# Gated linear attention with a spatially gated MLP: more kinds of work for ScalarE and GpSimd, and a new order of the whole program

## The chip, the cores and the metric

The kernel runs on one core of one Trainium2 chip. The metric is the device time of one execution in microseconds (us). The profile's names are used for the engines: PE is TensorE's matrix array, DVE is VectorE, ACT is ScalarE, POOL is GpSimd, SP is SyncE, which here only issues transfers (DMAs).

## The reference, cut to what matters

Batch 4, 8 heads, 768 steps, head size 40. The recurrent attention (below) feeds an MLP of 320 -> 1024 -> 320 columns with a mixing matrix over the 768 steps. All is float32.

```python
for t in range(S):
    m_new = np.maximum(f_gate[:, :, t] + m, i_gate[:, :, t])
    f_stab, i_stab = np.exp(f_gate[:, :, t] + m - m_new), np.exp(i_gate[:, :, t] - m_new)
    C = f_stab * C + i_stab * einsum('bhd,bhe->bhde', vt, kt)
    n = f_stab * n + i_stab * kt
    denom = np.maximum(np.abs(n . qt), 1.0)
    y[:, :, t] = sigmoid(o_gate[:, :, t]) * (C qt) / denom
h = np.maximum(x @ w_in, 0.0);  u, v = h[..., :512], h[..., 512:]
v_n = (v - mean(v)) / np.sqrt(var(v) + 1e-06)
v_s = einsum('ts,bsd->btd', w_spatial, v_n) + b_spatial
out = (u * v_s) @ w_out
```

## The kernel before, in words

The recurrence is computed in blocks of 128 steps for all 8 heads: 6 blocks a batch row, 24 blocks, numbered n = 0 to 23. Jobs are named by a short word and the number of the block:

- `s` (scores k.q, line 539), `ex` and `ebm` (the exponents of the decay as small matmuls, 542 and 551), on PE; `W` and `Eb` take their exponentials on ACT (554, 553).
- `ks` (two DVE products of `s` and `W`, 64 rows each) and `q` (two products of queries and `Eb`, on DVE or POOL) build the left operand of the output matmul. `kt` multiplies the keys by the last column of `W` (line 582); `dc` (PE, 578 and 580) makes from them what the block adds to the state; `c1`, `d1`, `d2`, `c2` carry the state on.
- `pv` (PE, 606 and 607) gives numerator and denominator. `da` takes twice the absolute denominator, `den` clamps it and takes the reciprocal (616, 617), `xm` multiplies `th` (the tanh form of the output gate) plus one by it (634), `xg` multiplies the numerator in, `xd` copies 64 columns, `px` (PE, 653) transposes, `xh` and `xl` store the result as a high and a low part, which together keep float32 in PE's fp32r format.
- In the MLP `V` (PE, 691) makes v, and `re`, `sq`, `va`, `po`, `nb`, `vn`, `vh`, `vl` normalise and split it; `pu` (733) and `u` make u; `pb` (743 to 745) is the mixing; `g`, `gu`, `gh`, `gl` gate and split; `c` (766 to 768) is the last matmul, `oc` and `out` copy and store. Names here carry batch row, half or block, and quarter: `V00`, `pu001`.

The weights must be split into high and low parts too. The input matrix comes in five pieces (`wi01`, `wi2`, `wi11`, `wi10`, `wi00`) whose words were viewed as 64-bit pairs, so the kernel first puts floats together: `_t` shifts one word right by 29 (line 427), `_x` rescales the other on ACT (429), `_b` merges both (431), `_h` rounds to the high part, `_l` takes the difference. The output matrix (`wo0` to `wo3`) goes the same way, the mixing matrix (`ws`) needs only `_h` and `_l`.

The gates are prepared on 32 partitions in three pieces of time, z = 0, 1, 2 (128, 256 and 384 steps): scan `m`, additions `fa`, `fs`, `is`, `as`, scan `g`, splits `gh`, `gl`, `ah`, `al`, nearly all on DVE. For block 0 four tiny transfers `dg0` to `dg3` and one `da` (same word as the denominator's job, without a number) carry them to the operands of `ex0`.

The order is written out by hand: the table ORDER lists every job, and each engine carries out its jobs in that order, one after the other. A suffix (`:V`, `:A`, `:P`) puts a job on DVE, ACT or POOL; without one the first engine in the job's list of alternatives takes it (a list like `dict(POOL=0.78, DVE=0.49)`, whose numbers are planned costs that the run does not use). Transfers go through the queues of SP and ACT in the same order, and a queue waits at the head for what its next transfer needs. Buffers come from pools (for instance 8 PSUM banks, 3 for q and k) and are handed out along the same table.

```python
job(f"kt{n}", dict(POOL=0.78, DVE=0.49), self.tt(...))
job(f"den{n}", dict(DVE=0.4), den1, w=[den], due=D0 + 6)
job(f"xm{n}", dict(POOL=1.85, DVE=0.485), gate, ...)
```

Of the kernel before, what the change touches and what calls it, by code (L numbers as in the profile page):

```python
# [9 lines left out]
F32 = mybir.dt.float32  # L10
# [3 lines left out]
AF = mybir.ActivationFunctionType  # L14
# [26 lines left out]
    ident=([128, 128], F32), warm=([128, 1], F32), half_neg=([128, 1], F32),  # L41
# [8 lines left out]
half_neg ident rhz1:V f1:A i0:S ey0:V f0:A rhz2:V i1 mk1 f2:A m0 wi01_ld cg0 mk0 i2 rst0 fa0 rst1 fs0 wi2_ld:A is0 g0 qk0:A m1 ca0 s0 gh0 dg1:A gl0 as0 wi01_t rhz0 dg0  # L50
rh0_1 ah0 rh0_0 fa1 dg2:A al0 wi2_x da dg3:A m2 fs1 wg0 wi2_t is2 is1 ex0 wi2_b wi11_ld:A g1 fa2 wi02_h as1 cg1 ah1 fs2 al1 gh1 qk1 W0 wi01_x wa1 cz0:V gl1 wg1 ks0_1
ks0_0 rh1_1:A ebm0 Eb0 kt0 dc0 ra01:A qk2 g2 wi01_b gm1 c1_0:A qz rh1_0 s1 as2 q0_1:V pv0 wi11_x gh2 gm2:A wi11_t ebm1 wi02_l wi10_ld d2_0 ex1 gl2 wi11_b ah2 th0 wg2 da0
den0 al2 wi11_h Eb1 W1 wa2 rh2_0 kt1 s2 dc1 wi10_x xm0:V wi11_l c2_0 ks1_0 rh2_1 gm3 qk3 wi00_ld d1_1:P xg0 ra02 xd0 ks1_1 ex2 c1_1 wi10_t q1_1:V q1_0 wi12_h eg01 ebm2
px0 wi10_b Eb2 th1 wi12_l xh0 xl0 wi10_h pv1 rh3_1:A da1 eg00 ebm3 gm4 eg11 W2 d2_1 qk4:A Eb3 wi10_l den1 kt2 xm1:V V00 ks2_1 xg1 rh3_0 ex3 c2_1 ks2_0 wi00_t wi00_x xd1
d1_2 q3_0:V wi00_b q2_1:V q2_0 rh4_0 px1 ebm4 xh1 rh4_1 W3 ex4 W4 wi01_h kt3 re00 dc2 c1_2 s3 d2_2:P pv2 xl1 dc3 s4 wi01_l:P da2 Eb4 gm6 gm5 th2 ks3_0 V01 ks3_1 c2_2 d1_3
qk5 ey1 den2 c1_3 ws00_ld:A ebm5 xm2:V we0 ex5 ks4_1 ca1 d2_3:P wa0 xg2 kt4 c2_3 q3_1:V ra10 xd2 rh5_1 ks4_0 q4_0:V d1_4:P wi00_h px2 eg20 gm7:A eg10 W5 q4_1:V dc4 s5 pv3
c1_4 xh2 pv4 sq00 th4 th3 xl2 ks5_1 we1 d2_4:P V02 ks5_0 wi00_l:P va00:V qk6:A re01 da3:V wo0_ld:A Eb5 rh5_0 pu001 ws00_h ex6 den3 xm3:V re02 c2_4 q5_0:V da4 ra11 th5
den4 eg21 po00 sq01 W6 rh6_0 pu002 pu000 xm4:V rh6_1:A u001 kt5:V q5_1:V eb7_1 xg4 xd4:V px4 dc5 va01:V qk7 xg3 nb00 d1_5 xd3:P vn00 s6 vh00:V xh4 c1_5 xl4 vl00 wo0_x
eb6_0 u000 sq02 pv5 ks6_1 da5:V ra22:A px3 po01 den5 va02:V ws00_l:P nb01:V V04 xh3 ex7 xl3 xm5:V po02 vn01 ks6_0 ws02_ld eb6_1 ws01_ld re04 xg5 W7 nb02:V u002 cz6 q6_1
xd5:V eb7_0:A V03 px5 vn02 sq04 kt6:V dc6 s7 c1_6:A va04 po04 xh5 nb04 ws01_h vh02 vn04 gm9 wo3_ld pv6 ws02_h:V gm8 xl5 vh01:V ks7_1 da6 re03 ks7_0 V05 vl01 vh04:V vl04  # L60
ws02_l:P ws01_l:P wo1_ld rh7_0 vl02 sq03 re05 va03 po03 pb0030 th6 pu003 sq05 va05 po05 nb05 pb0031 wo1_t we2 pb0032 ra12 d2_6:P u003 nb03:V wo1_x vn03 rh8_0 q7_1:V
# [145 lines left out]
class Kernel:  # L207
# [294 lines left out]
    def attention(self, n):  # L502
# [334 lines left out]
```

## Time and profile before

| | us |
|---|---|
| three runs, median (lowest to highest) | 348.05 (347.5 to 350.71) |
| the profiled execution, its own time | 346.94 |
| its span, first to last instruction | 345.2 |
| PE busy in the span | 326.2 |
| DVE / ACT / POOL busy | 257.6 / 130.7 / 108.7 |

A matmul's end is modelled, so a busy PE is not PE at its peak; the distance from one start to the next says at which rate it works. Idle time is put down to what released the waiting instruction.

### The profile page before, as it was taken

What the parts mean: (1) busy time and instruction counts of PE and PEld (TensorE: products, weight loads), DVE (VectorE), ACT (ScalarE), POOL (GpSimd) and SP (SyncE); (2) the same over time, 40 slices, a digit from 0 to 9 for tenths busy, and PEclk for the clock granted to TensorE, in tenths of its full rate; (3) what the DMA queues carried; (4) which work ended last, traced back from release to release, by engine and by line L of the source; (5) the groups of instructions that cost most, each with busy time, mean ns of one, the idle gap of its engine ahead of it and who ended that gap; (6) DMA issues with size and microseconds to landing.
All of it is one profiled execution on the core that took longest, in us unless ns stands there. A gap on an engine that the chain in (4) does not pass through costs nothing.

```text
span 345.2 us, 9069 instructions
## 1 busy us (share of the span) xinstructions
PE 326.2 (95%) x3654; PEld 303.7 (88%) x3654; DVE 257.6 (75%) x545; ACT 130.7 (38%) x312; POOL 108.7 (32%) x154
## 2 busy tenths in 40 slices
PE   0499999999899999999999999999999999999995
PEld 0387788899899989999999989999999999999995
DVE  5999998789997979865569657696946785536471
ACT  1455576961541166550221146640112227402011
POOL 6123553746643013434051005440233612100000
PEclk9999999999999999999999999999999999999999
DMA  6879658878373493250703674242061000100012
GB/s 194 229 213 264 175 161 226 213 160 225 120 226 99 130 230 91 62 150 0 211 26 96 177 184 113 68 124 78 10 160 38 0 3 21 58 0 2 0 40 76
DMA packets 17866, 40.12 MB, mean 116 GB/s; under 512 B 4212, under 2 KB 7860, under 8 KB 17824
## 3 DMA queue, kind: packets, MB, share of 16 engines
q1 hardware_dynamic: 12048, 26.49, 28.1%
q10 hardware_dynamic: 5616, 12.94, 13.8%
q8 instruction: 29, 0.48, 0.6%
q0 software_dynamic: 160, 0.11, 0.2%
q14 instruction: 13, 0.11, 0.1%
HBM read 35.09 MB, written 4.42 MB: 114 GB/s over the span
## 4 chain that ended last, share of the span: by engine, by line
PE 71%; DVE 4%; issue 1%; ACT 1%
PE pu L733 11%; PE pm L691 10%; PE pb L743 9%; PE pb L745 8%; PE pb L744 8%; PE pc L766 4%; PE pc L768 4%; PE pc L767 4%; PE pv L606 4%; PE s L539 3%; PE dc L578 2%; PE px L653 2%; DVE pb L255 1%; DVE KS L255 1%; PE pv L607 1%
## 5 line engine op out<-in xcount | busy, mean ns | idle before, releaser
L743 PE MATMUL pb<-wsH,v 128*128 128x384 f32 x192 | 65.6, 342 | 0.2 <-DVE KS L255 0.2
L745 PE MATMUL pb<-wsH,v 128*128 128x384 f32 x192 | 64.7, 337 | 0.0
L744 PE MATMUL pb<-wsL,v 128*128 128x384 f32 x192 | 64.6, 337 | 0.0
L539 PE MATMUL s<-QK 40*64 40x64 f32 x768 | 29.6, 232 | 10.2 <-DMA QK<-in_qk 10.2
L743 PEld LDWEIGHTS pb<-wsH,v 128*128 128x128 f32 x192 | 36.1, 188 | 0.9 <-issue 0.5
L744 PEld LDWEIGHTS pb<-wsL,v 128*128 128x128 f32 x192 | 36.1, 188 | 0.5
L255 DVE TENSOR_TENSOR KS<-s,W 64x512 f32<-64x512 f32 x48 | 33.0, 688 | 4.6 <-PE s L539 2.3
L745 PEld LDWEIGHTS pb<-wsH,v 128*128 128x128 f32 x192 | 36.0, 188 | 0.0
L539 PEld LDWEIGHTS s<-QK 40*64 40x64 f32 x768 | 26.4, 145 | 10.6 <-DMA QK<-in_qk 10.2
L255 DVE TENSOR_TENSOR pb<-pb,bsp 128x384 f32<-128x384 f32 x32 | 17.7, 562 | 22.3 <-PE pb L745 22.2
L733 PE MATMUL pu<-xH,wiH 128*128 128x384 f32 x96 | 32.9, 342 | 0.6 <-ACT W L554 0.6
L733 PE MATMUL pu<-xL,wiH 128*128 128x384 f32 x96 | 32.3, 336 | 0.0
L259 ACT CAST gt<-pb 128x384 fp32r<-128x384 f32 x21 | 10.0, 481 | 57.2 <-DVE pb L255 49.4
L766 PE MATMUL pc<-woH,gt 128*128 128x320 f32 x96 | 30.5, 318 | 0.0
L255 POOL TENSOR_TENSOR KS<-QK,Eb 64x512 f32<-64x512 f32 (+1 forms) x21 | 27.7, 1318 | 8.1 <-PE pc L768 6.2
L691 PE MATMUL pm<-wiH,xH 128*128 128x512 f32 x72 | 29.9, 416 | 0.0
L767 PE MATMUL pc<-woL,gt 128*128 128x320 f32 x96 | 29.7, 309 | 0.0
L768 PE MATMUL pc<-woH,gt 128*128 128x320 f32 x96 | 29.6, 309 | 0.0
L691 PE MATMUL pm<-wiH,xL 128*128 128x512 f32 x72 | 29.0, 403 | 0.0
L607 PE MATMUL pv<-RH,KS 128*64 128x41 f32 x384 | 27.4, 237 | 1.2 <-DVE RH L255 0.7
L606 PE MATMUL pv<-RH,KS 104*64 104x41 f32 x384 | 27.8, 238 | 0.4 <-DVE gt L255 0.4
L606 PEld LDWEIGHTS pv<-RH,KS 104*64 104x64 f32 x384 | 25.4, 145 | 2.8 <-issue 1.2
(124 smaller groups left out, 761.5 us busy)
## 6 DMA issues: line engine op xcount, KB each, us to landing
RH<-in_vk SPq DMA_DIRECT2D x35, 256.0 KB
QK<-in_qk SPq DMA_DIRECT2D x15, 448.0 KB
QK<-in_qk ACTq DMA_DIRECT2D x9, 448.0 KB
RH<-in_vk ACTq DMA_DIRECT2D x13, 256.0 KB
out<-o SPq DMA_DIRECT2D x14, 160.0 KB
wsr<-in_w_sp SPq DMA_DIRECT2D x5, 384.0 KB
out<-o ACTq DMA_DIRECT2D x10, 160.0 KB
wir<-in_w_in SPq DMA_DIRECT2D x3, 512.0 KB
```

The lines of the kernel that those rows point to most:

```text
L255: return lambda e: e.tensor_tensor(out=out(), in0=in0(), in1=in1(), op=op)
L539: self.nc.tensor.matmul(o[64 - p0:128 - p0, h], q[p0:p0 + D, 0, h], q[p0:p0 + D, 1, h], start=True, stop=True)
L606: self.nc.tensor.matmul(o[0:64, h], ks[0:ke, 0, h], v0[0:ke, h], start=True, stop=True)
L607: self.nc.tensor.matmul(o[64:128, h], ks[:, 1, h], v1[:, h], start=True, stop=True)
L691: self.nc.tensor.matmul(pmt(), l, r, start=i == 0, stop=i == len(terms) - 1)
L733: self.nc.tensor.matmul(put(), w, x, start=i == 0, stop=i == len(terms) - 1)
L743: self.nc.tensor.matmul(pbt(), vH[:, cd], wh[:, s], start=s == 0, stop=False)
L744: self.nc.tensor.matmul(pbt(), vH[:, cd], wl[:, s], start=False, stop=False)
L745: self.nc.tensor.matmul(pbt(), vL[:, cd], wh[:, s], start=False, stop=s == NB - 1)
L766: self.nc.tensor.matmul(pct(), gH[:, c], wh[:, d], start=d == 0, stop=False)
L767: self.nc.tensor.matmul(pct(), gH[:, c], wl[:, d], start=False, stop=False)
L768: self.nc.tensor.matmul(pct(), gL[:, c], wh[:, d], start=False, stop=d == 3)
```

## The change

Four jobs get a further engine, and the table ORDER is replaced as a whole (all its 1,587 entries in another sequence, with other suffixes (before 1,586)).

- `_t`, the shift, may run on ACT: the top byte is read as uint8, scaled by 1/32, with a bias that makes the rounding give the floor. ACT gets 4 of the 5 shifts of `wi` and 2 of the 4 of `wo`.
- `kt` may run on ACT as eight instructions, one for each head, with the scale read from `W`. ACT gets it for n = 2, 4, 8, 23; DVE has 7 in place of 9, POOL 13 in place of 15.
- `den` may run on POOL, as the clamp and a power of -1 (exponent tile `neg`, a new constant). POOL gets 11 of 24: n = 4, 5, 10, 11, 12, 14 to 19.
- `xm` may run on ACT as eight instructions with scale and bias read from `den`: n = 8, 12, 23. DVE has 15 in place of 20, POOL 6 in place of 4.

```diff
-        job(name + "_t", fast(n), lambda e: e.tensor_scalar(
-            out=raw()[:, :, 0], in0=raw()[:, :, 0], scalar1=29, scalar2=None, op0=ALU.logical_shift_right), w=[(rb, 0)], due=due + 2)
+        def top(e):
+            lo = raw()[:, :, 0]
+            if e is self.nc.scalar:
+                byte = raw().rearrange("p n w -> p (n w)").bitcast(mybir.dt.uint8).rearrange("p (n w) -> p n w", w=8)[:, :, 3]
+                e.activation(out=lo, in_=byte, func=AF.Copy, scale=1.0 / 32, bias=-31.0 / 64)
+            else:
+                e.tensor_scalar(out=lo, in0=lo, scalar1=29, scalar2=None, op0=ALU.logical_shift_right)
+        job(name + "_t", {**fast(n), **act(n + 70)}, top, w=[(rb, 0)], due=due + 2)
...
+        def weigh(e):
+            if e is self.nc.scalar:
+                for h in range(H):
+                    e.activation(out=self.rh_k(n)[:, h], in_=self.rh_k(n)[:, h], func=AF.Copy, scale=self.T(W)[:, h, L - 1:L])
+            else:
+                e.tensor_tensor(out=self.rh_k(n), in0=self.rh_k(n), in1=self.T(W)[:, :, L - 1:L].broadcast_to([128, H, D]), op=ALU.mult)
+        job(f"kt{n}", dict(POOL=0.78, DVE=0.49, ACT=1.7), weigh, r=[W], w=[(RH, ("k", 0)), (RH, ("k", 1))], due=D0 + 1.5)
...
         def den1(e):
             e.tensor_scalar_max(out=dt_(), in0=dt_(), scalar1=2.0)
-            e.reciprocal(out=dt_(), in_=dt_())
+            if e is self.nc.gpsimd:
+                e.tensor_tensor(out=dt_(), in0=dt_(), in1=F("neg").t, op=ALU.pow)
+            else:
+                e.reciprocal(out=dt_(), in_=dt_())
...
-            if e is self.nc.gpsimd:
+            if e is self.nc.scalar:
+                for h in range(H):
+                    e.activation(out=hd(xt())[:, h], in_=hd(self.rh_o(n))[:, h], func=AF.Identity, scale=dt_()[:, h:h + 1], bias=dt_()[:, h:h + 1])
+            elif e is self.nc.gpsimd:
```

```diff
 ORDER = """
-half_neg ident rhz1:V f1:A i0:S ey0:V f0:A rhz2:V i1 mk1 f2:A m0 wi01_ld cg0 mk0 i2 rst0 fa0 rst1 fs0 wi2_ld:A is0 g0 qk0:A m1 ca0 s0
+f0 ident i0 rst0 rhz0:V m0 i1 f1:A cg0 rhz1:V fa0 fs0 mk1 mk0 rst1 is0 g0 as0 m1 neg qk0 f2 s0 qz:V ey1 i2 rh0_0:A gh0 ah0 wi01_ld
```

Three places show what the table moves. The first is SP's queue from its start: `ft` and `it` are the gates, `wir` a piece of the input matrix, `GM<-gp` and `AT<-ap` the tiny transfers `dg` and `da` for block 0, `RH` the values and keys of a block, `QK` its queries and keys. Before:

```order
L338 DMA it<-in_i_gate 32x128
L445 DMA wir_112<-in_w_in 128x1024
L386 DMA GM_72<-gp_152 1x8x64
L499 DMA RH_76<-in_vk 64x1024 x2
L390 DMA AT_73<-ap_161 16x1x128
L394 DMA scr_g<-gp_152 32x4x64
```

Now:

```order
L338 DMA ft<-in_f_gate 32x128
L523 DMA QK_127<-in_qk 112x1024
L338 DMA ft<-in_f_gate 32x384
L454 DMA wir_155<-in_w_in 128x1024
L387 DMA GM_73<-gp_151 1x8x64 x2
L391 DMA AT_74<-ap_153 16x1x128
L395 DMA scr_g<-gp_151 32x4x64
L508 DMA RH_77<-in_vk 64x1024
```

The forget gate's first piece and block 0's queries and keys (before on ACT's queue, behind seven other transfers) now open SP's queue, and `da` stands ahead of the `RH` loads.

The second place is DVE up to the first product `ks0` (`KS<-s,W`); `mt` and `gc` are the two scans, `gp` and `ap` the split results. Before:

```order
L431 SCALAR_TENSOR_TENSOR wir_126<-wir_126 128x512
L359 SCALAR_TENSOR_TENSOR gc<-rst,ft 32x256
L351 TENSOR_TENSOR ft<-ft,mt 32x384
L255 TENSOR_TENSOR it<-it,gc 32x256
L356 TENSOR_TENSOR ft<-ft,mt 32x384
L255 TENSOR_TENSOR ap_186<-it,ap_186 32x256
L565 MEMSET RH_76 40x328
L255 TENSOR_TENSOR gp_190<-gc,gp_190 32x2x128
L255 TENSOR_TENSOR KS_86<-s_135,W_194 64x512 x2
```

Now:

```order
L360 SCALAR_TENSOR_TENSOR gc<-rst,ft 32x256
L352 TENSOR_TENSOR ft<-ft,mt 32x384
L255 TENSOR_TENSOR it<-it,gc 32x256
L255 TENSOR_TENSOR gp_184<-gc,gp_184 32x2x128
L357 TENSOR_TENSOR ft<-ft,mt 32x384
L255 TENSOR_TENSOR it<-it,mt 32x384
L255 TENSOR_TENSOR ap_190<-it,ap_190 32x256
L583 TENSOR_TENSOR RH_77<-RH_77,W_194 128x320
L255 TENSOR_TENSOR KS_87<-s_130,W_194 64x512 x2
```

No weight work (`wir`) stands ahead of `ks0` any more, and `kt0` (`RH<-RH,W`), before on POOL, now stands on DVE just ahead of it.

The third place is POOL in the first batch row, where `st` is the normalisation's statistics and `den` the denominator of blocks 5 and 4:

```order
L721 TENSOR_SCALAR st_722<-st_722 128x1
L723 TENSOR_TENSOR st_722<-st_722,half_neg 128x1
L630 TENSOR_SCALAR den_707<-den_707 128x8
L632 TENSOR_TENSOR den_707<-den_707,neg 128x8
L724 TENSOR_SCALAR st_588<-st_588 128x1
L724 TENSOR_SCALAR st_722<-st_722 128x1
L630 TENSOR_SCALAR den_864<-den_864 128x8
L632 TENSOR_TENSOR den_864<-den_864,neg 128x8
```

The four `den` rows are new on POOL; before, a clamp and a reciprocal stood on DVE.

## Rows read from the trace of the kernel before

**Rows 1.** Busy time by stretch; columns: stretch, length, each engine's busy us, PEclk, DMA share, GB/s.
```profile
10.00:25.00 15.00, 11.99 (x172) 9.69 (x174) 14.36 (x31) 7.46 (x16) 2.25 (x4) 1.00 0.79 220
25.00:35.00 10.00, 10.00 (x82) 7.24 (x76) 9.62 (x20) 5.71 (x15) 3.96 (x4) 1.00 1.02 263
35.00:55.00 20.00, 18.71 (x336) 15.88 (x335) 19.10 (x43) 13.31 (x34) 9.30 (x12) 1.00 0.65 181
...
75.00:100.00 25.00, 24.13 (x331) 23.09 (x330) 23.92 (x46) 9.56 (x21) 14.92 (x13) 1.00 0.59 171
100.00:341.60 241.60, 241.36 (x2494) 229.65 (x2493) 167.93 (x356) 76.77 (x188) 59.26 (x89) 1.00 0.30 82
```

**Rows 2.** PE's waits: who waited for whom, us in total, times, longest.
```profile
PE s L539 <- DMA QK<-in_qk: 10.2, 1, 10.2
...
PE ex L542 <- DMA AT<-ap: 1.3, 1, 1.3
```

**Rows 3.** Timeline of PE, matmuls V at 31 and at 62 us: start, us.
```profile
31.43 0.63 PE L691 MATMUL pm<-wiL,xH 128*128 128x512 f32 x1
31.85 0.63 PE L691 MATMUL pm<-wiH,xL 128*128 128x512 f32 x1
...
61.98 0.40 PE L691 MATMUL pm<-wiL,xH 128*128 128x512 f32 x1
62.22 0.39 PE L691 MATMUL pm<-wiH,xL 128*128 128x512 f32 x1
```

**Rows 4.** Timeline of the start, 4 to 38 us: start, us, [idle before, releaser].
```profile
4.29 0.69 DVE L343 TENSOR_TENSOR_SCAN mt<-ft,it 32x128 f32<-32x128 f32 x1 [1.66 <-DMA ft<-in_f_gate]
...
8.83 0.28 DVE L255 TENSOR_TENSOR ap<-it,ap 32x128 fp32r<-32x128 f32 x1 [0.99 <-ACT ap L259]
...
9.23 0.78 SPq L390 DMA_DIRECT2D AT<-ap  x1
...
14.96 0.58 ACT L554 ACTIVATE W<-ex 128x512 f32<-128x512 f32 x1
15.08 0.41 DVE L255 TENSOR_TENSOR gp<-gc,gp 32x256 fp32r<-32x256 f32 x1 [0.26 <-ACT gp L259]
...
15.57 1.39 DVE L255 TENSOR_TENSOR KS<-s,W 64x512 f32<-64x512 f32 x2
...
37.56 0.48 DVE L255 TENSOR_TENSOR RH<-dc,ta 40x328 f32<-40x328 f32 x1
```

**Rows 5.** DVE by operation and shape: xcount, busy us, mean ns, idle before.
```profile
L255 DVE TENSOR_TENSOR KS<-QK,Eb 40x512 f32<-40x512 f32 x10 | 8.8, 877 | 0.3
...
L616 DVE TENSOR_SCALAR den<-den 128x8 f32<-128x8 f32 x24 | 5.4, 224 | 0.3
...
L617 DVE RECIPROCAL den<-den 128x8 f32<-128x8 f32 x24 | 4.9, 203 | 0.8
L255 DVE TENSOR_TENSOR RH<-RH,W 128x320 f32<-128x320 f32 x9 | 4.3, 483 | 0.1
...
L431 DVE SCALAR_TENSOR_TENSOR wir<-wir 128x512 uint32<-128x512 uint32 x5 | 3.4, 675 | 0.0
...
L427 DVE TENSOR_SCALAR wir<-wir 128x512 uint32<-128x512 uint32 x5 | 2.1, 417 | 0.0
...
L255 DVE TENSOR_TENSOR wiL<-wir,wiH 128x512 fp32r<-128x512 f32 x2 | 1.4, 683 | 0.0
...
L322 DVE MEMSET RH<- 32x328 f32 x2 | 0.7, 332 | 0.2
```

**Rows 6.** POOL and ACT by operation and shape, the same columns.
```profile
L703 POOL TENSOR_TENSOR st<-st,half_neg 128x1 f32<-128x1 f32 x24 | 14.1, 587 | 25.8 <-DVE st L701 12.8 <-DVE den L616 11.9
...
L255 POOL TENSOR_TENSOR wiL<-wir,wiH 128x512 fp32r<-128x512 f32 x2 | 2.6, 1304 | 0.2
...
L709 ACT ACTIVATE pm<-pm,st 128x512 f32<-128x512 f32 x16 | 12.0, 751 | 3.5 <-DVE st L704 3.5
...
L259 ACT COPY x<-x 128x64 f32<-128x64 f32 x8 | 2.0, 246 | 10.3 <-DVE x L255 10.3
```

More of the change, by code (lines that the diff above doesn't have):

```diff
@@ L53 @@
-den0 al2 wi11_h Eb1 W1 wa2 rh2_0 kt1 s2 dc1 wi10_x xm0:V wi11_l c2_0 ks1_0 rh2_1 gm3 qk3 wi00_ld d1_1:P xg0 ra02 xd0 ks1_1 ex2 c1_1 wi10_t q1_1:V q1_0 wi12_h eg01 ebm2
-px0 wi10_b Eb2 th1 wi12_l xh0 xl0 wi10_h pv1 rh3_1:A da1 eg00 ebm3 gm4 eg11 W2 d2_1 qk4:A Eb3 wi10_l den1 kt2 xm1:V V00 ks2_1 xg1 rh3_0 ex3 c2_1 ks2_0 wi00_t wi00_x xd1
-d1_2 q3_0:V wi00_b q2_1:V q2_0 rh4_0 px1 ebm4 xh1 rh4_1 W3 ex4 W4 wi01_h kt3 re00 dc2 c1_2 s3 d2_2:P pv2 xl1 dc3 s4 wi01_l:P da2 Eb4 gm6 gm5 th2 ks3_0 V01 ks3_1 c2_2 d1_3
@@ L104 @@
-c312 oc34:V out34:A oc33 c313 out33 oc31 out31:A
+f0 ident i0 rst0 rhz0:V m0 i1 f1:A cg0 rhz1:V fa0 fs0 mk1 mk0 rst1 is0 g0 as0 m1 neg qk0 f2 s0 qz:V ey1 i2 rh0_0:A gh0 ah0 wi01_ld rhz2:V gl0 wi2_ld:A al0:P ca0 ey0 dg1
+dg0 da dg3:A dg2:A ex0 fa1 m2 is1 fs1 wg0 g1 cg1 fa2 as1 rh0_1 wa0 wi11_ld:A gh1 gl1 wg1 ebm0 ah1 fs2 is2 W0 Eb0 cz0 q0_1 al1 kt0:V qk1 wi2_t:A dc0 wa1 gm1:A rh1_0 ks0_0
+ks0_1 c1_0:A wi2_x g2 gh2 wi11_t pv0 s1 gm2 qk2 as2 wi01_t:A wi11_x ra01 gl2 wi2_b d2_0 ah2 al2 wi12_h:V rh1_1:A eg00 da0 th0 ebm2 wi01_x wg2 den0 wi12_l wa2 wi02_h ebm1
@@ new lines @@
+wi01_b xm0:V rh2_0:A Eb1 wi11_b q1_1:V rh2_1:A ex2 q1_0:V ex1 c2_0 W1 eg01 kt1 xg0 wi10_ld xd0 rh3_0:A ks1_0 gm4 ra02 wi11_h gm3 ks1_1 s2 dc1 wi10_t:A wi10_x d1_1:P c1_1
+px0 wi11_l pv1 ex4 d2_1 W2 Eb2 qk3 wi02_l:P wi00_ld xh0 wi10_b wi10_h:V kt2:A ebm3 rh3_1 wi10_l:P xl0 ks2_1 ks2_0 ebm4 qk4 q2_0 c2_1 th1 da1 den1 xm1:V xg1 Eb3 V00 ex3
+ca1 q3_0:V q2_1:V th2 q3_1:V rh4_0 xd1 W4 d1_2:P px1 W3 xh1 dc2 c1_2 s3 wi00_x half_neg xl1 wi00_t:A pv2 rh4_1 kt3 d2_2 dc3 s4 V01 da2 Eb4 gm5 wi01_h wi00_b c2_2 den2
@@ L294, in consts @@
         job("half_neg", dict(DVE=0.06), lambda e: e.memset(F("half_neg").t, -0.5), w=[F("half_neg")], due=-3)
+        job("neg", dict(DVE=0.08, POOL=0.15), lambda e: e.memset(F("neg").t, -1.0), w=[F("neg")], due=-3)
         job("warm", dict(ACT=0.22), lambda e: e.activation(out=F("warm").t, in_=F("half_neg").t, func=AF.Exp), r=[F("half_neg")], w=[F("warm")], due=-2)
@@ L636, in attention @@
         job(f"da{n}", dict(ACT=0.19, DVE=0.37), den0, r=[pv], w=[den], due=D0 + 6)
-        job(f"den{n}", dict(DVE=0.4), den1, w=[den], due=D0 + 6)
-        job(f"xm{n}", dict(POOL=1.85, DVE=0.485), gate, r=[den], w=[(x, 0), (RH, ("o", 0)), (RH, ("o", 1))], due=D0 + 6)
+        job(f"den{n}", dict(DVE=0.4, POOL=0.85), den1, r=[F("neg")], w=[den], due=D0 + 6)
+        job(f"xm{n}", dict(POOL=1.85, DVE=0.485, ACT=1.7), gate, r=[den], w=[(x, 0), (RH, ("o", 0)), (RH, ("o", 1))], due=D0 + 6)
         job(f"xg{n}", dve(320), self.tt(lambda: hd(xt()), lambda: pvt()[:, :, 0:D], lambda: hd(xt()), ALU.mult), r=[pv], w=[(x, 0)], due=D0 + 6)
@@ L653, in trans @@
                 self.nc.tensor.transpose(p[:, j], self.T(x)[:, j * 128:(j + 1) * 128], F("ident").t)
[L655 removed]
+        job(f"xd{n}", dict(ACT=0.246, POOL=0.24, DVE=0.19), self.cp(lambda: self.T(x)[:, DM:384], lambda: self.T(x)[:, 256:DM]), r=[(x, 0)], w=[(x, 1)], due=D0 + 7)
         add(f"px{n}", dict(PE=0.328), trans, r=[x, F("ident")], w=[px], mode="M", due=D0 + 8.0, hold=[xH, xL])
```

113 lines of the change are left out of this document (54 added, 59 removed).

## The prediction

> **What bounds the kernel now.** I read the busy time by stretch first, then PE's waits, then the timeline of the start, then the groups of instructions by shape. From 100 us to its last matmul PE is busy 241.36 of 241.60 us; from 75 to 100 it idles 0.87, from 35 to 55 it idles 1.29, while before 35 us it idles all of the first 10.2 (PE's longest wait, for block 0's queries and keys) and 3.0 of the next 15 [rows 1, 2]. So from 35 us on there are only about 2.2 us to be had by any order, and the rest of the loss lies at the start. There DVE is the full engine: 14.36 of 15, 9.62 of 10 and 19.10 of 20 us busy from 10 to 55, while POOL is busy 2.25 of the 15 and 3.96 of the 10, and ACT about half [rows 1]. PE is called busy in those stretches, but it works in small pieces, each waiting for DVE's next product.
>
> The start is also slow on PE itself. V's matmuls start 0.42 us apart at 31 us and 0.24 apart at 62 us [rows 3], though the granted clock reads 1.00, full speed, in both stretches [rows 1]. [...]
>
> **The sum runs against the profiled execution**, 346.94 us with a span of 345.2. The median of the three runs is 348.05, 1.1 above it; I carry the difference over to the median.
>
> **Part 1, up to the first product.** Before, DVE's first scan m0 starts at 4.29 after 1.66 of waiting, and ks0 at 15.57, which is 11.28 later, 1.25 of it idle (0.99 and 0.26) [rows 4]: 10.03 of work. Taken out of this stretch: two shifts at 0.417, one merge at 0.675, al0 at 0.28, one zeroing at 0.332, together 2.12 [rows 4, 5]. Put in: two zeroings at 0.332, which lay in the wait before m0 until now, a third over 512 columns (0.5, estimated from the 0.332 for 328), and the tiny constant neg (under 0.1), together 1.2. Work becomes 9.1. m0 itself starts earlier, because f0 is first in its queue and not second: bounds 0 and the 1.66 that DVE waits there; I take 0.5, about one issue. DVE is thus free for kt0 at 3.8 + 9.1 = 12.9.
>
> kt0 needs W0, which started at 14.96 [rows 4]; ex0 in front of it waited for the transfer da, 1.3 us of it plain [rows 2], and da was issued at 9.23, behind two RH loads in SP's queue and after DVE's late ap [rows 4]. Now as0, ah0 and al0 stand right behind the scan, so da can be issued some 1.5 us sooner, with the loads behind it. What its landing costs in the new company the trace doesn't show: bounds for W0 are 14.96 (nothing won) and 12.0; I take 2.0 us, W0 at 13.0, since both causes of delay go. DVE then has kt0 at 13.0. The move of queries and keys to the head of SP's queue frees s0 from its 10.2 us, but that alone wins nothing: ex0 came after it anyway.
>
> **Part 2, from ks0 to the state of block 2.** c1_2, which pv2 waits for, ends at 38.04 [rows 4]. From ks0's start DVE does 22.47 us without a gap. Taken out: two shifts at 0.417, two differences at 0.683 (wi02_l and wi10_l go to POOL), a merge at 0.675 that now comes later, d1_2 at 0.5, together 3.4; one 64-row product q leaves and one enters. Put in: kt0 0.483, a merge 0.675 from part 1, two casts of weights (0.42 each, as the shift over the same columns), a 40-row product q1_0 at 0.877, together 2.9 [rows 5]. So 22.0, and c1_2 could end at 13.0 + 22.0 = 35.0, which is 3.0 earlier.
>
> Two things eat from that. wi10_l, which V00 needs, takes 1.304 on POOL where DVE took 0.683 [rows 5, 6], and V00's eight slow matmuls, px1 and dc2 must still come before c1_2. I take 0.4 off: 2.6 us at pv2. The two orders have done the same PE work by then, so it is a true lead.
>
> **Part 3, after pv2.** PE is nearly full from there, so the lead should last to the end; the pattern at the end (c, oc, out) is unchanged. Of PE's 2.2 us of idle time [rows 1] I count 0.5 as won, because DVE gets lighter until 100 us: it loses 11 of 24 den (0.224 + 0.203 each [rows 5], 4.7 us), five xm and two kt, and takes more casts. Against it stand the new forms:
> - Shift on ACT: one pass over 512 columns, nearest rows ACT's copies; ACT had room.
> - kt and xm in eight steps. A copy of 64 columns took 0.246 [rows 6], so eight cost at least about 2.0; a 512-column step with scale and bias from memory took 0.751 [rows 6], so at most 6.0. I take 2.2, nearer the first row, as 40 columns are short. Only kt2 (near 28 us) and kt4 lie where ACT is full: th1 and da1 queue behind kt2, and DVE's den1 behind those. I count 0.3 us against; with 6.0 it would be 4.
> - den on POOL. A power over one column took 0.587 [rows 6]. If most of that is fixed, eight columns and the clamp cost 0.8; if each column costs it, 4.7 and more. I take 0.8, since POOL's work on whole rows is far cheaper per column (1.304 for 512 [rows 6]). Between pv10 and px10, the tightest place, stand two other pv, one pu and two pb, over 4 us of PE work, which cover 0.8 but not 4.7.
> - More work on POOL beside DVE. DVE's 40-row product of two SBUF tensors took 0.877 on average where the 512-column difference took 0.683 [rows 5]. I count 0.2 us against, since most of the added POOL work lies after 100 us, where DVE is busy 168 of 242 us [rows 1].
>
> [...]
>
> Sum: 2.6 + 0.5 - 0.3 - 0.2 = 2.6 us. The profiled execution would take 344.3, the median 345.4.
>
> **The rivals.**
> - A larger gain (A). Part 2's 3.0 is reached in full, PE works densely enough from pv1 on to go to its fast step before V00 (8 x 0.18 = 1.5 us saved), and 1.5 of the 2.2 idle us go: 6 us, 342.0. For it speaks that before V00 ex4 and ebm4 now fill gaps; against it that those too are held by DVE. [...]
> - No lead (B). The small transfers land no sooner: W0 stays at 14.96, DVE stands still for 1.9 us more, and 0.7 of the 2.6 is left: 347.3. For it: the DMA share from 10 to 35 us is 0.79 to 1.02 [rows 1], so a small transfer sits among big ones, and all five weight and block loads are still wanted then.
> - Slower (C). The power on POOL costs its one-column price for every column. den then takes 4.7 + 0.2 where DVE took 0.43, and n = 10, 5 and 16 overrun the PE work in between by some 2 us each; den4 and den5, den10 and den11, den15 and den16 stand in pairs on POOL, so the second of each waits 4 more. 6 + some 3 for pairs, less the 2.6: 354. It decides from about 3 us per den on. The same place would give it if the eight steps on ACT cost 6 us.
>
> **How the numbers follow.** Forecast 0.48, A 0.27, B 0.15, C 0.10. One per cent, 3.5 us, is about what a measurement of this kernel can tell from no change. The forecast's own range, 344 to 347, lies within it but for its lower end (0.07 of its 0.48); A is faster, B is the same, C is slower. Hence faster 0.34, same 0.56, slower 0.10. The range goes from A's 342 to where B and half of C's way lie, 349.5; beyond its ends I leave some 0.05 below and 0.1 above.
>
> **What would show it.** Right: PE's longest wait (for QK) near 5 us, W0 near 13, ks0 near 13.5, c1_2's end near 35.4, V00 near 29.5, PE idle after 35 us at most 2 us, and den on POOL about 0.8. Wrong: W0 still at 14.9 (B); V's first matmuls 0.24 apart (A); a power of several us on POOL, with PE waiting for px (C); or new idle time on PE after 100 us, where I expect none.

## The result: one per cent slower

The changed kernel takes 350.78 us (median of 20 runs, 349.46 to 355.72), the kernel before 347.31 beside it (20 runs, 346.04 to 352.12). The ratio is 1.0105, with a 95% interval from 1.0078 to 1.0132: slower by about 3.5 us. All ratios leave out runs that fell into a slower state, here one of the changed kernel's 20, while the medians are of all runs. I had forecast 345.4 and a range up to 349.5; the time lies outside it.

The profiled execution of the changed kernel is 354.38 us (span 352.6), 3.6 above its median. A second profile (the first experiment) is 351.50 us (span 349.7), nearer to the typical run; where the two differ, the text says which one is meant.

Busy time by stretch of the first profile, with the columns of [rows 1]:

```profile
10.00:25.00 15.00, 10.52 (x126) 7.91 (x128) 12.52 (x26) 8.54 (x19) 2.11 (x3) 1.00 0.88 235
...
55.00:75.00 20.00, 17.61 (x285) 14.96 (x283) 17.02 (x34) 11.37 (x27) 15.66 (x21) 0.94 0.67 181
...
100.00:348.00 248.00, 244.53 (x2509) 231.34 (x2508) 165.04 (x331) 89.20 (x228) 80.56 (x109) 1.00 0.31 81
```

DVE did become lighter (12.52 of 15 us where [rows 1] had 14.36), as planned. But behind 100 us PE idles 3.47 us, where it idled 0.24 before, and between 55 and 75 it idles 2.39 with a granted clock of 0.94. PE's waits name the places (columns as in [rows 2]):

```profile
PE ex L551 <- DMA GM<-gp: 5.6, 1, 5.6
PE s L548 <- DMA QK<-in_qk: 5.2, 1, 5.2
PE pv L620 <- issue: 1.6, 1, 1.6
PE pu L753 <- DVE x L255: 1.6, 2, 1.1
PE dc L592 <- DVE RH L583: 1.5, 1, 1.5
PE ex L551 <- DMA GM<-scr_g: 1.4, 1, 1.4
PE pc L786 <- DVE KS L255: 0.9, 1, 0.9
```

The first two are the old start, split: the scores wait 5.2 instead of 10.2 [rows 2], and the exponents then wait for the gates' row. Of the five below, the one of dc stood there before too (1.6 us); the other four are new, 5.5 us together. Apart from pu's two, each is one place.

The start, in the form of [rows 4]:

```profile
2.56 0.41 DVE L344 TENSOR_TENSOR_SCAN mt<-ft,it 32x128 f32<-32x128 f32 x1 [1.37 <-DMA it<-in_i_gate]
...
7.64 0.72 SPq L391 DMA_DIRECT2D AT<-ap  x1
8.82 0.34 SPq L395 DMA_DIRECT2D scr_g<-gp  x1
11.12 0.57 SPq L508 DMA_DIRECT2D RH<-in_vk  x1
...
13.56 0.60 ACT L563 ACTIVATE W<-ex 128x512 f32<-128x512 f32 x1 [0.36 <-PE ex L551]
...
15.21 0.49 DVE L583 TENSOR_TENSOR RH<-RH,W 128x320 f32<-128x320 f32 x1 [1.56 <-DMA RH<-in_vk]
15.62 1.40 DVE L255 TENSOR_TENSOR KS<-s,W 64x512 f32<-64x512 f32 x2
```
and one of the waits of SP's own queue up to 16 us:
```profile
SPq L508 <- DMA GM<-gp: 1.9, 1, 1.9
```

m0 is 1.7 us earlier than in [rows 4], da (AT<-ap) 1.6, W0 1.4. Then kt0 (L583) stands 1.56 us for block 0's values, whose second half was asked for only at 11.12, and ks0 starts at 15.62, as late as before (15.57); in the second profile it is 16.62. Of the load's lateness 1.9 us are not its place in the order: at the head of SP's queue it stood until the tiny transfer GM<-gp had landed, of which it reads nothing.

The forms whose price had been open (the first block by tile: count, duration min/median/max in ns, first and last start; the second by shape, as in [rows 5, 6]):

```profile
L630 DVE TENSOR_SCALAR den<-den x13: 152/172/396, 21.4 to 297.9; 128x8 f32<-128x8 f32 x13
...
L630 POOL TENSOR_SCALAR den<-den x11: 237/248/562, 55.4 to 257.3; 128x8 f32<-128x8 f32 x11
L632 POOL TENSOR_TENSOR den<-den,neg x11: 1661/1679/1867, 55.7 to 257.6; 128x8 f32<-128x8 f32 x11
```
```profile
L649 ACT ACTIVATE x<-RH,den 128x40 f32<-128x40 f32 x24 | 7.8, 408 | 3.0 <-DVE den L634 2.5 <-POOL den L632 0.5
L581 ACT ACTIVATE RH<-RH,W 128x40 f32<-128x40 f32 x32 | 7.4, 314 | 0.5 <-ACT woH L259 0.5
```

A den costs 0.25 + 1.68 = 1.93 us on POOL. A kt in eight steps is 7.4/4 = 1.9 us on ACT, an xm 7.8/3 = 2.6.

**A view that adds up.** To see where time is lost for good, I took each group of PE's matmuls in the order of the program and subtracted from its start the work that stands ahead of it, with the same fixed time for each kind in every kernel (scores 0.90 us, V 1.85, pu 1.395, a pb 0.525, a sum pv 0.95, and so on, each near its fast duration). What is left is how far PE lags behind its own work; it rises only where PE stands or steps slowly, and two kernels compare at the same amount of work done. Each column is one profile:

```
PE work done, us   before   changed (2nd)   early load   +4 den   +2 waits   +spread
  12                24.7        27.1           24.6        24.5      25.3      25.4
  36                28.5        30.7           28.2        26.7      27.5      27.5
  44                28.8        31.2           29.6        28.2      29.7      28.4
  60                29.9        32.0           29.7        28.4      29.9      28.8
  90                31.7        33.9           32.4        29.2      30.6      29.4
 120                33.0        35.7           34.2        31.0      31.2      30.1
 150                33.3        36.8           35.4        32.1      32.5      31.3
 180                34.5        39.0           37.6        34.3      33.4      32.1
 310                36.1        40.7           39.3        36.0      35.2      33.9
```

The changed kernel's second profile is 2.4 us behind the kernel before at work 12 (the state of block 2) and loses 2.3 more between 90 and 180. The columns to the right are the experiments that took the losses away one by one.

### The profile page after: what moved, and what is told of

Same layout as the page of the kernel before. It is cut to its first block, busy times and chain, and to the rows that moved or that the text cites. A ratio compares the mean times of both kernels' runs of the same rounds, so it can differ in the third digit from the quotient of the medians.

```text
span 352.6 us, 9098 instructions
## 1 busy us (share of the span) xinstructions
PE 329.9 (94%) x3654; PEld 305.0 (87%) x3654; DVE 249.7 (71%) x507; ACT 146.8 (42%) x374; POOL 128.0 (36%) x177
## 4 chain that ended last, share of the span: by engine, by line
PE 81%; POOL 6%; DMA 4%; DVE 4%; issue 2%; SPq 0%; ACT 0%; POOLq 0%; DVEq 0%
PE pu L753 11%; PE pb L763 9%; PE pm L711 9%; PE pb L764 9%; PE pb L765 9%; PE s L548 6%; PE pv L620 5%; PE pc L786 4%; PE pc L788 4%; PE pc L787 4%; PE dc L592 4%; POOL den L632 3%; DMA GM<-scr_g 2%; PE ex L551 2%; PE px L673 2%; PE pv L621 2%
## 5 line engine op out<-in xcount | busy, mean ns | idle before, releaser
L255 POOL TENSOR_TENSOR KS<-QK,Eb 64x512 f32<-64x512 f32 (+1 forms) x22 | 28.7, 1310 | 5.5 <-DMA QK<-in_qk 2.7
L711 PE MATMUL pm<-wiH,xL 128*128 128x512 f32 x72 | 29.8, 414 | 0.2 <-DVE xL L255 0.2
L621 PEld LDWEIGHTS pv<-RH,KS 128*64 128x64 f32 x384 | 25.3, 145 | 2.8 <-issue 2.0
```

The source lines that it names most:

```text
L255: return lambda e: e.tensor_tensor(out=out(), in0=in0(), in1=in1(), op=op)
L621: self.nc.tensor.matmul(o[64:128, h], ks[:, 1, h], v1[:, h], start=True, stop=True)
L711: self.nc.tensor.matmul(pmt(), l, r, start=i == 0, stop=i == len(terms) - 1)
```

## The experiments

Two theories stood at first. START: the lead is lost at ks0, by the late load. POWER: the lead is eaten behind 55 us, by the powers on POOL. All edits but the two on the kernel before are moves or engine letters in the order's table, shown as tokens of it.

**The changed kernel again.**

> The changed kernel once more, to have a profile nearer to its typical run than the one of 354.38 us, and as the base for the three runs beside it. Every theory: 350.8 +- 0.6, ratio to the kernel before 1.010. In the profile, if the stall of 1.6 us in front of pv6 at 70 us and the clock of 0.94 behind it belong to the kernel, they are here too; if they were an accident of one execution, V05 runs at its fast step and the span is some 3.5 us shorter than 352.6.

Measured: 351.50 us in the profile, 352.44 median of 4, ratio 1.0106 (1.0034 to 1.0178). The pause in front of the last sums of pv6 is not here, and V05 runs at its fast step: so the 1.6 us at 70 us and the slow clock behind it are not in every execution. They come back below.

**All den on DVE.**

```diff
-... den4:P ... den5:P ... den10:P ... (eleven)
+... den4 ... den5 ... den10 ...
```

> All 11 den that the change put on POOL go back to DVE, nothing else is touched. Theory POWER (the power on POOL, 1.93 us per den against 0.43 on DVE, is what eats the gain from 55 us on): the waits of PE behind den4, den5 (0.7 each), den10 and den11 (1.3) go, together 2 to 3 us: 348 to 349. Theory START (the change loses because its lead is gone at ks0, and den lies beside PE's work): 350.8 or, as DVE gets 4.7 us more to do, up to 351.5.

Measured: 355.51 us, ratio 1.0181 (1.0102 to 1.0261). Both theories missed: it is slower, not faster. PE's waits, and one stretch of its windows:

```profile
PE pv L620 <- DVE KS L255: 4.6, 2, 2.4
```
```profile
255.00:260.00 5.00, 3.85 (x86) 3.78 (x88) 4.66 (x13) 0.00 (x0) 0.00 (x0) 0.53 0.05 17
```

PE's 1.1 us for pu at n = 10 is gone, as POWER says. But this order puts den19 on DVE ahead of block 20's key products. DVE stands 2.76 us for pv19's sum ahead of den19, pv20 waits for those products 2.35 us, and PE's clock then falls to 0.53. So in this order den19 on DVE holds up the key products behind it. Moving all eleven back is no measure of the power.

**Block 0's second load early.**

```diff
-qz:V ey1 i2 rh0_0:A gh0 ... as1 rh0_1 wa0
+qz:V ey1 i2 rh0_0:A rh0_1 gh0 ... as1 wa0
```

> Block 0's second load of values is issued right behind the first, ahead of the small transfers of gates, instead of behind them, where the queue stood for 2 us. Theory START: kt0 on DVE starts near W0 (13.7 instead of 15.2) and ks0 near 14.2; 1.3 us are won there and stay: 349.5. Theory POWER: kt0 comes earlier all the same, but what is won before 55 us is lost at the waits behind den, less than 0.4 us at the end: 350.4 to 350.8.

```profile
2.10 0.55 SPq L508 DMA_DIRECT2D RH<-in_vk  x1
...
14.14 0.49 DVE L583 TENSOR_TENSOR RH<-RH,W 128x320 f32<-128x320 f32 x1 [0.62 <-ACT W L563]
```

Measured: 350.39 us, ratio 1.0056 (1.0015 to 1.0097). kt0 now waits for W0 alone, and in the lag view the changed kernel's 2.4 us at work 12 are gone. Of them 1.4 are left at the end of this profile; the medians put the gain at 0.4 us, the ratios at 1.7, and their intervals overlap. So START is real, but how much of it lasts was not settled here.

**Both edits together.**

> Both edits, den on DVE and the early load. If the two losses are separate: the sum of both, 346.5 to 347.5, so no slower than the kernel before. If they share their cover (a lead that the waits behind den would have eaten): 348 to 349, as with den on DVE alone.

Measured: 355.49 us, ratio 1.0149 (1.0047 to 1.0251). Neither sum holds: the stands behind the eleven den cover everything, as in the run with den alone.

**Only four den on DVE.** Now the lag view chose the den: those behind which it rose (n = 4, 5, 10 and 11).

```diff
-... den4:P ... den5:P ... den10:P ... den11:P
+... den4 ... den5 ... den10 ... den11
```

> Early load as in the run before, and only den4, den5, den10 and den11 back on DVE; den12 and den14 to den19 stay on POOL, where the trace shows no new wait of PE behind them. With all eleven back DVE stood behind sums that were not there yet (new waits at 144, 192 and 254 us). Theory PRICE (a power of 8 columns takes 1.68 us, and it costs where PE has little other work: 0.7 + 0.6 at n = 4, 5 and 1.35 at n = 10, 11): 350.4 - 2.6 = 347.8. Rival PLACE (any den moved in this order makes DVE stand, the engine is not the point): 351 to 355, as with all eleven.

Measured: 348.12 us, ratio 1.0010 (0.9973 to 1.0047), below the early load alone by 2.3 in the medians and 1.6 in the ratios; PRICE had said 347.8. In the lag view the gain over the early load sits where these four stand: 1.4 us between work 12 and 36 and 1.9 between 60 and 90. What stood there in the changed kernel's second profile, on POOL and on DVE:

```profile
118.20 1.68 POOL L632 TENSOR_TENSOR den<-den,neg 128x8 f32<-128x8 f32 x1
```
```profile
119.92 0.49 DVE L654 SCALAR_TENSOR_TENSOR x<-RH,den 128x320 f32<-128x320 f32 x1 [4.60 <-POOL den L632]
```

DVE stands 4.6 us, the last 1.7 of them for this one power. The gate's product comes then, pv10's bank is free only behind it, and pu011 wants a bank.

**Two waits more.**

```diff
-V14 d2_13 ks14_0 ks13_1
+V14 ks14_0 ks13_1 d2_13
-pv15 oc12 da15 ... vh21 gm19 V20
+pv15 oc12 gm19 da15 ... vh21 V20
```

> The same, and two waits more taken away: the gate rows of block 19 are asked for before out11 and five loads of values and not behind them (PE stood 0.77 for them at 210 us, and lost 0.95), and on DVE the second product of block 13's keys is put ahead of the decay product (1.41 us beside POOL's three products instead of 0.50), for which c040 waited 0.87 and lost 1.03. Theory WAITS (the loss behind 100 us is a handful of single waits, and nothing takes their place): 347.8 - 2.0 = 345.8, faster than the kernel before. Rival COVER (what is won is lost at the next such place): 347.4 to 347.8.

Measured: 345.62 us, ratio 0.9934 (0.9900 to 0.9969): faster than the kernel before, and 0.2 from WAITS. In the lag view this profile is 1.4 us behind the one with four den at work 90 and 0.9 ahead at 180, so the gain lies where the two edits are. The decay product in the changed kernel's second profile, with POOL's products beside it, and then here:

```profile
145.72 3.90 POOL L255 TENSOR_TENSOR KS<-QK,Eb 40x512 f32<-40x512 f32 x3
```
```profile
148.59 1.39 DVE L255 TENSOR_TENSOR tb<-RH,Eb 40x328 f32<-40x328 f32 x1
```
```profile
146.59 0.49 DVE L255 TENSOR_TENSOR tb<-RH,Eb 40x328 f32<-40x328 f32 x1
```

Behind POOL's row the same product takes 0.49, and by then nobody waits for it.

**The kernel before with the eleven den on POOL.** Constant, power and engine as in the change (den1 as in the change's diff), the old order kept.

```diff
+job("neg", ...)
-job(f"den{n}", dict(DVE=0.4), den1, w=[den], due=D0 + 6)
+job(f"den{n}", dict(DVE=0.4, POOL=0.85), den1, r=[F("neg")], w=[den], due=D0 + 6)
-half_neg ident rhz1:V ... den4 eg21 ... den5 va02:V
+half_neg ident neg rhz1:V ... den4:P eg21 ... den5:P va02:V
```

> The kernel before, with its own order, and only the eleven den on POOL. Theory PRICE: 1.5 us more per den wherever PE runs short of other work, so a loss of 1 to 4 us: 349 to 351. Rival (hidden: DVE is lighter by 4.7 us, PE has other work): 346.8 to 347.8.

Measured: 357.85 us, ratio 1.0258 (1.0181 to 1.0335). The direction is PRICE's, the size is not. In the trace:

```profile
63.10 1.84 POOL L255 TENSOR_TENSOR wsL<-wsr,wsH 128x768 fp32r<-128x768 f32 x1
```
```profile
63.16 2.13 DVE L638 SCALAR_TENSOR_TENSOR x<-RH,den 128x320 f32<-128x320 f32 x1 [1.35 <-POOL den L619]
```
```profile
66.34 0.44 PE L657 MATMUL px<-ident,x 128*128 128x128 f32 x2 [1.69 <-DVE x L255]
```
```profile
65.00:70.00 5.00, 2.88 (x57) 2.42 (x59) 3.38 (x7) 2.11 (x5) 4.08 (x7) 0.70 0.94 258
70.00:75.00 5.00, 5.00 (x54) 4.32 (x51) 4.76 (x8) 3.54 (x9) 3.52 (x4) 0.50 0.85 193
```

The late den pushes DVE's gate product beside POOL's weight difference, where it takes 2.13 instead of 0.49; PE stands 1.69 and then 0.78 for the two px, its clock falls to 0.50, and the lag grows by 7.6 us between work 32 and 40. Two prices of 1.5 us have become more than 7.

**The kernel before with nine den on POOL** (n = 4 and 5 back on DVE).

```diff
-... den4:P eg21 ... den5:P va02:V
+... den4 eg21 ... den5 va02:V
```

> The kernel before with nine den on POOL: n = 4 and 5 are back on DVE, the rest as in the run with eleven, which took 357.85 and whose trace puts the loss at 64 to 80 us (PE stood 1.69 and 0.78 for px4 and px5, and its clock then fell to 0.50 for five us). Theory PLACE AND CLOCK (two dens did it, by the stand and by the slow clock behind it): 348 to 349.5. Rival PRICE ALONE (each den its share): 355 to 356.

Measured: 353.53 us, ratio 1.0134 (1.0069 to 1.0199): between the two. The loss at 64 to 80 us is gone from the trace (the lag grows 0.5 between work 32 and 44), so it was those two den. But this profile lags 4 us already at work 16, ahead of any den on POOL: its scores at 38 us step at half speed, where the kernel before is at full speed.

```profile
38.72 1.70 PE L540 MATMUL s<-QK 40*64 40x64 f32 x28
```
```profile
36.54 1.03 PE L539 MATMUL s<-QK 40*64 40x64 f32 x29
```

Why its fast step came some 9 us later (at about 43 us and not 34) is open, and so is what the other nine den cost by themselves.

**No eight steps on ACT** (early load; kt2, kt4, kt8, kt23, xm8, xm12, xm23 on DVE).

```diff
-wi10_h:V kt2:A ebm3 ... th3 xd2 kt4:A ... pb0100 xm8:A xg7
+wi10_h:V kt2:V ebm3 ... th3 xd2 kt4:V ... pb0100 xm8:V xg7
```

> Early load as before, and the seven jobs in eight steps (kt2, kt4, kt8, kt23, xm8, xm12, xm23) on DVE instead of ACT. Theory STEPS (eight steps of 1.9 to 3.2 us on ACT hold up what comes behind): 0.3 to 1 us faster, 349.4 to 350.1. Theory FREE (they lie where ACT has room, and DVE is short of time before 40 us): the same or up to 0.7 slower, 350.4 to 351.1.

Measured: 352.25 us, ratio 1.0106 (1.0043 to 1.0169), 1.9 slower than with the steps. Not STEPS; FREE has the sign, but had said 0.7 at most. Some of the 1.9 need not be the steps: in this profile V05 runs partly at the slow step (0.43 us from start to start), behind a pause of PE that is the subject of the next run. And the order was written for these steps on ACT, so, as with all eleven den on DVE, this is no measure of what they cost against the kernel before.

**Block 8's scores behind V05.** Seven of the eight profiles of the new order had, by now, a pause of PE in the middle of pv6, of 0.9 to 1.7 us, with nothing missing that the profile shows. The version with two waits less, its PE row and one of the DMA queues of 66.5 to 69.5 us:

```profile
69.23 0.20 PE L620 MATMUL pv<-RH,KS 104*64 104x41 f32 x1 [1.61 <-issue]
```
```profile
q8 instruction: 1, 0.02, 2.1%
```

Queue 8 is of kind instruction, where the queues with the loads are of kind hardware_dynamic: 29 transfers, 0.48 MB, in the whole span, one for every 126 of PE's 3,654 matmuls on average, and one starts at 66.94 us, shortly ahead of the pause.

```diff
-V04 eb7_1:A re04 nb03 sq04 dc6 s8 dc7 s7 ... pv6 ... V05 q7_1
+V04 eb7_1:A re04 nb03 sq04 dc6 dc7 s7 ... pv6 ... V05 s8 q7_1
```

> The best version so far (345.62 us), with block 8's scores behind V05 instead of ahead of pv6, so that PE no longer runs five groups of 32 short matmuls (dc6, s8, dc7, s7, pv6) in a row. In seven of the eight profiles of the new order PE stands for 0.9 to 1.7 us at its matmul 845 or 846, in the middle of pv6, with no data missing; the transfer of kind instruction that starts just before starts with PE at matmul 800 to 830, and PE goes on 2.3 to 2.7 us after that start; in the one profile without the pause it started with PE at matmul 776. Theory FETCH (PE outruns the loading of its own instructions there): the pause goes or is under 0.3 us, 344.2 to 344.8. Rival (the pause is of the place in time or of pv6 itself): it stays, 345.6.

Measured: 344.63 us (344.29 to 345.31, 7 runs), ratio 0.9899 (0.9863 to 0.9935): faster than the kernel before by 1%, and 1.0 below the version with the pause. The pause is gone. The transfer now starts with PE at its matmul 796, by count 49 ahead of matmul 845, and not at 830, 15 ahead of it; PE comes to matmul 845 (now one of s8) 3.4 us after the start. This is as FETCH says, and pv6 itself is still there, so it wasn't the cause by itself. PE's waits of this version:

```profile
PE s L548 <- DMA QK<-in_qk: 5.5, 1, 5.5
PE ex L551 <- DMA GM<-gp: 5.4, 1, 5.4
PE pv L621 <- DVE RH L255: 0.6, 1, 0.6
PE dc L592 <- DVE RH L583: 0.5, 1, 0.5
```

Only the start is left. **That move alone in the changed kernel:**

> The changed kernel with that one move alone. Theory FETCH: the pause of up to 1.6 us at 70 us goes, and with it the lower clock that followed it in the profile of 354.38 us; as one of the two profiles of the changed kernel had no such pause, 0.8 to 1.3 us in the median: 349.5 to 350.0. Rival: 350.8.

Measured: 350.19 us, ratio 1.0077 (1.0049 to 1.0105), 0.6 below the changed kernel (1.0 by the ratios, whose intervals overlap) and between the two forecasts. The pause is gone here too, as in all four profiles with this move; while eight of the nine profiles of the new order without it have one.

**The early load taken out again** (from the version at 345.62).

```diff
-rh0_0:A rh0_1 gh0 ... as1 wa0
+rh0_0:A gh0 ... as1 rh0_1 wa0
```

> The best version so far without its early load of block 0's values, which stands behind the small transfers again. Theory START (the order's lead at the start is lost by this load): kt0 at 15.2 or later and 1.4 to 2 us slower than with it, 347.0 to 347.6. Rival (pauses of PE behind 60 us take up the difference either way): 345.6 to 346.2.

Measured: 347.03 us, ratio 0.9972 (0.9940 to 1.0003): 1.4 slower than with it, as START says. Once the later waits are gone, the start's loss shows in full. Its profile bears on FETCH as well: the pause is there, 0.87 us, although the transfer had started with PE at matmul 751, earlier than the 776 of the one profile without a pause. So the count at the start doesn't decide; but this transfer took 1.6 us where most take about 1.0, and counted from its end this profile is like the others (below).

**Why there is hardly a lead at block 2.** In the best version DVE has done its row by 36.45 us (34.45 + 2.00), but c1_2 starts at 37.55:

```profile
31.72 0.80 PE L711 MATMUL pm<-wiH,xH 128*128 128x512 f32 x1
...
35.73 0.84 PE L673 MATMUL px<-ident,x 128*128 128x128 f32 x3
36.50 0.29 PE L592 MATMUL dc<-RH 64*40 64x41 f32 x1
```
```profile
34.45 2.00 DVE L255 TENSOR_TENSOR KS<-QK,Eb 40x512 f32<-40x512 f32 x3
37.55 0.49 DVE L255 TENSOR_TENSOR RH<-dc,ta 40x328 f32<-40x328 f32 x1 [1.09 <-POOL RH L583]
```

(The row names POOL, whose kt3 ended at 37.50; but c1_2 doesn't need it, as in the profile below it starts 0.4 before kt3 ends. What c1_2 adds is dc2, which PE starts at 36.50; its last sum ends 0.1 before c1_2 in both profiles.) The profile with the early load alone has the same order up to here, and V00 at 31.60, but PE reaches its fast step right behind V00, ahead of px1:

```profile
35.44 0.49 PE L673 MATMUL px<-ident,x 128*128 128x128 f32 x3
```
```profile
36.78 0.49 DVE L255 TENSOR_TENSOR RH<-dc,ta 40x328 f32<-40x328 f32 x1 [0.45 <-issue]
```

There c1_2 is 0.8 us earlier than in the best version and in the kernel before. So it is PE's slow step that holds c1_2; why the fast step comes sooner in one profile than in another is open.

Two runs asked whether V00 comes late because of the difference on POOL:

```diff
-wi10_l:P
+wi10_l:V
```

> The best version (344.63 us) with the one difference wi10_l back on DVE (0.68 instead of 1.30 us on POOL). Theory POOL DIFFERENCE (V00 waits for it): V00 starts at 31.1 instead of 31.7, c1_2 at 37.2 instead of 37.55, 0.3 us faster: 344.3. Rival DVE FULL (my forecast: DVE's row of work sets c1_2): 0.7 us later, 345.3.

```diff
-c1_1 px0 wi11_l pv1 ex4 d2_1 W2 ... xh0 wi10_b wi10_h:V kt2:A
+c1_1 wi10_b wi10_h:V px0 wi11_l pv1 ex4 d2_1 W2 ... xh0 kt2:A
```

> The best version with the weight's merge and cast (wi10_b, wi10_h) ahead of two other jobs on DVE, so that POOL can begin wi10_l at about 29.7 instead of 30.4. Theory POOL DIFFERENCE: V00 at 31.2, held then by xl0 on DVE, c1_2 at 37.2: 344.2 to 344.4. Rival DVE FULL: DVE stands up to 0.6 us for the product on ACT ahead of the merge and c1_2 comes that much later: 344.6 to 345.2.

Measured: 345.85 us, ratio 0.9969 (0.9931 to 1.0007), and 345.74, ratio 0.9946 (0.9918 to 0.9974): both slower than the best version, by 1.2 and 1.1 in the medians. DVE FULL has the direction, but both are slower than it said, and c1_2 starts at 37.85 and 37.93. V00 starts at 31.44 and 31.57, hardly earlier, so the difference on POOL isn't what holds it: between pv1 and V00 PE has work of its own, at slow steps (the two eb at 30.29 take 1.22 us). And DVE lost a microsecond each time beside POOL: in the first of the two runs on the weight's cast, in the second on the decay product tb (1.50 us at 30.16, where the best version took 0.49). The weight's cast with POOL at work (first two rows), and without (third, the best version):

```profile
29.25 1.38 POOL L255 TENSOR_TENSOR KS<-QK,Eb 40x512 f32<-40x512 f32 x1 [1.71 <-ACT Eb L562]
```
```profile
29.53 1.38 DVE L259 CAST wiH<-wir 128x512 fp32r<-128x512 f32 x1
```
```profile
29.81 0.43 DVE L259 CAST wiH<-wir 128x512 fp32r<-128x512 f32 x1
```

**The account.** From the changed kernel to the best version, by the medians (and by the ratios): early load 0.4 (1.7), four den 2.3 (1.6), two waits 2.5 (2.6), the spread 1.0 (1.2), together 6.2 (7.2). If the four are counted as losses of the new order, the rest of it is worth about 3 us; no run took that rest by itself. None of the four is a matter of how much work an engine has in all.

## Why the prediction was wrong

**What bounds the kernel** was read rightly: nothing to be had behind 35 us but some 2 us (my own rows add up to 2.4, not 2.2), the rest at the start. What I drew from it was not. "Nearly full" meant that any new wait of PE there costs its whole length, and I looked for gains in that stretch, not for new waits.

**Part 1** (kt0 at 13.0). m0 came at 2.56, better than my 3.8, DVE was free for kt0 at 13.64 against 12.9, and W0 came at 13.56 against 13.0. The step that failed is "with the loads behind it": I took the loads that da was moved past as free, while kt0 needs both halves of block 0's values. The second half was issued at 11.12 and kt0 began at 15.21 (16.21 in the second profile). Before, both halves had stood ahead of da; that was why da was late, and also why kt0 was not. A smaller slip: I let kt0 begin with W0, though it needs W0's end, 0.6 later. With the early load kt0 starts at 14.14, which is W0's end.

**Part 2** (c1_2 at 35.0, a lead of 2.6 at pv2). DVE's row was sized nearly right: from kt0 at 14.28 to 36.45 in the best version, 22.2 us, or 22.7 with c1_2, which my 22.0 includes. The step that failed is "I take 0.4 off" for V00's slow matmuls, px1 and dc2: once DVE is early, PE at its slow step is the bound. DVE stands 1.1 us for dc2 in the best version, and c1_2 starts at 37.55, where it started at 37.56 before [rows 4]. Only where PE's fast step came sooner was the wait 0.45, near my 0.4, and 0.8 of the 2.6 was there (36.78, and 36.7 to 36.8 in two more profiles). In the others it is B's outcome, though not B's reason, since W0 did come sooner. A's fast step ahead of V00 did not come: V00's matmuls start 0.42 to 0.43 us apart in the changed kernel as in the best version, and no run shows that denser work brings the fast step forward.

**Part 3.**
- den on POOL: 1.93 us against my 0.8, between the bounds 0.8 and 4.7 that I had. If the time grows evenly with the columns, which I estimate from these two widths alone, the row of one column (0.587 [rows 6]) is mostly fixed, but seven more columns add 1.1, some 0.16 each, so of the 1.68 for eight most goes with the columns. The mis-sized term cost 2.3 us (1.6 by the ratios).
- Rival C had the place right (pv10 to px10, and the pair at n = 4, 5), but not the point from which it decides: I wrote 3 us per den, and 1.93 was enough. I had counted PE's other work there as cover ("over 4 us"), without the other things in the queues ahead of the gate's product, which POOL's den now makes late.
- Eight steps: 1.9 us for a kt, near my 2.2, and 2.6 for an xm. The 0.3 that I counted against them was not measured by itself; in this order they are better than DVE, without them the kernel is 1.9 us slower.
- POOL beside DVE: my 0.2 was an average, and on average it was about even: in the second profile the 40-row products take 754 ns (877 before [rows 5]) and DVE's kt 705 (483 before). The 877 was no even price: eight of the ten products took 0.68 to 0.70 us with POOL busy beside them for 0.2 us at most, and two, at 78.60 and 94.70, took 1.12 and 2.14 beside POOL's weight differences. And a single product, d2_13 at 1.39 instead of 0.49, stood where PE waited and cost 1.0. The cast, 1.38 against 0.43, has one input; I had priced two-input products only. Which of DVE's instructions POOL slows, and why, no run settles.
- "New idle time on PE after 100 us, where I expect none" was my own sign of being wrong, and it came: 3.47 us instead of 0.24. The gate rows of block 19 behind five big loads, and the pause at 70 us, I had not looked for at all.

**The numbers.** The chance of slower by over 1% was 0.10, all of it on one mechanism. That mechanism cost about 2 us, far less than C's 6 to 9; being slower by one per cent took it and three losses that I had put at nothing or nearly nothing. In a kernel with PE at 99.9% of a stretch, a new order has more ways to lose than to win, and the range should have reached to 352.

## What to carry to other kernels

Where one engine is full, judge a new order by the waits that it puts on that engine, one by one, and not by how much lighter the others become; the lag of PE behind its own work shows in one column where each is lost. Moving a load behind something urgent delays whoever reads it (here kt0, at 15.21 us and at 14.14 with the load early): look for the reader before calling the move free. And a slow operation put on an idle engine is priced by what its consumer's queue holds up, not by the idle engine's time: in the best version PE waits for none of the seven den left on POOL, while the same 1.9 us cost over a microsecond at n = 10.

## What the runs showed of the hardware that I had not expected

**PE can pause with no data missing that the profile shows.** A row of some 160 short matmuls (five groups of 32, some 0.03 us each at 66 us) ran into a pause of 0.87 to 1.67 us in eight of nine profiles; in seven of them PE goes on 2.3 to 2.7 us after the transfer of kind instruction starts (66.94 to 69.23 above), in the eighth, with the late load, 3.4. From the transfer's end it is 1.2 to 1.7 us in all eight (there the transfer ended at 67.93), and in the new order's five profiles without a pause PE comes to the same matmul by count 1.2 us or more after the end: in none of the thirteen does it get there sooner. With 32 of these matmuls moved away there is none in four of four. That PE waits here for its own instructions fits every profile; but it was not shown: it is argued from the times and from the transfer's kind, as no run moved the transfer alone. What makes the transfer start when it does is open.

**Slow steps can follow a pause.** Behind the 1.62 us pause V05 ran at the slow step; behind one of 1.61, in another version, it did not:

```profile
73.07 0.63 PE L711 MATMUL pm<-wiH,xL 128*128 128x512 f32 x1
73.50 0.63 PE L711 MATMUL pm<-wiH,xH 128*128 128x512 f32 x1
```
```profile
70.27 0.40 PE L711 MATMUL pm<-wiH,xL 128*128 128x512 f32 x1
70.51 0.40 PE L711 MATMUL pm<-wiH,xH 128*128 128x512 f32 x1
```

The first steps 0.43 us, the second 0.24. The length of the pause alone doesn't decide: of the five profiles with a pause of 1.15 us or more, four have V05 at the slow step at least in part; of the three with less than 1 us, none. Over 20 us the granted clock only hints at it (0.94 for 55 to 75). In the first profile's worst 2 us it tells, 0.50:

```profile
74.00:76.00 2.00, 2.00 (x7) 1.61 (x6) 1.78 (x3) 0.13 (x1) 0.00 (x0) 0.50 0.38 135
```

But at the start it read 1.00 beside slow steps [rows 1, 3], so the steps are the surer sign.
